# Second products by token tile at the end of the MLP, a new order in the first projections, and four steps to placing, in an attention and MLP kernel

## The chip, the cores and the metric

The kernel runs on one core of a Trainium2 chip. The metric is the device time of one execution in microseconds (us), taken as the median of the runs.

## The reference

A pre-norm attention layer with residual is followed by a pre-norm MLP with residual, for 2048 tokens of 512 features, 32 heads of 16 features, and 1792 hidden features.

```python
def _A_ref(x, wqkv, wo):
    qkv = (x @ wqkv).reshape(B, S, 3, H, Dh).transpose(2, 0, 3, 1, 4)
    q, k, v = qkv[0], qkv[1], qkv[2]
    scores = einsum("bhqd,bhkd->bhqk", q, k) * Dh ** -0.5
    p = softmax(scores, axis=-1)
    o = einsum("bhqk,bhkd->bhqd", p, v)
    return o.transpose(0, 2, 1, 3).reshape(B, S, D) @ wo

def _B_ref(x, w1, w2):
    h = silu(einsum("bsd,df->bsf", x, w1))
    return einsum("bsf,fd->bsd", h, w2)

h = x + _A_ref(layernorm(x), wqkv, wo)
h2 = h + _B_ref(layernorm(h), w1, w2)
```

## The kernel before

**Numbers.** Large products are made of fp16 halves: an operand is split in a high and a low part, and high by high, high by low and low by high are added in PSUM. So each product of 128 rows has three matmuls. The helpers are `mm` (L98, a matmul), `tr` (L101, a transpose on TensorE), `pool`, `act`, `dve` and `dma` (L105, L112, L115, L118: an operation on GpSimd, ScalarE, VectorE, and a DMA issued by SyncE); nearly every row of the profile has one of these lines, and the names of its tiles tell what it is. All of them keep the order of the program on their engine.

**Stages.** The first projections (0 to about 181 us) normalize the tokens in four blocks b of 512, project q and k (`project_qk`, L581) and v (`project_v`, L610, token tile by token tile of 128) and store q and k split, 48 rows for each head: `qs` for queries, `ks` for keys. Units of a block are n = 0 and 1 (k, then q, of two groups of heads) and n = 2 to 5 (token tiles of v). The weights' low parts (`wqk_l`, `wv_l`) are made by `split_qk` and `split_scaled` (L538) in between, the statistics and the norm of the next block by `statistics` and `normalize`.

Attention follows in 512 steps g. A step belongs to an item i = g // 16 (four heads and 512 queries), c = g % 16. It has four score matmuls (`scores`, L453: keys by queries, `ps<-qs,ks`), four exps on ScalarE (`pt<-ps`, 128 x 512), and the PV matmuls of the step two before (`values`, `ps<-pt,va`). The maximum of each query's scores is found ahead of the item: the scores of a later item are made the other way round (`ps<-ks,qs`) and reduced by VectorE (`mx`, L293 for one, L291 for a pair of banks), up to three maxima in a step, 64 for each item. `maxima(g)` (L1223) says how many a step gets, from the maxima still missing until each item begins; `BESIDE` (L72) says how many are made inside each of the three MLP blocks.

**Placing.** When the last maximum of a piece is found (`found_maxima`, L384), GpSimd splits the negative maxima in fp16 (`finish_max`, L300), and they are placed as two rows for each head into `qs`, which makes the score matmul subtract them. A piece is an item, or half of the last one: (31, 0) and (31, 1). If it is early enough, `place_far` (L330) does so `CALM` steps later: a DVE transpose `mt<-ns`, four DMAs to DRAM, and two DMAs `qs<-md`. Otherwise `place_max` (L342) does so two steps after: a transpose on TensorE into a bank of the scores, a DVE copy `mn<-ps`, and two DMAs `qs<-mn` (L354), both issued by SyncE. 27 pieces go the first way; items 8, 16, 24, 30 and both halves of 31 go the second.

**MLP.** The 2048 tokens go in four blocks of 512. Three are done inside the attention, ahead of steps 144, 272 and 400 (about 475 to 577, 838 to 941, 1199 to 1297 us), by `mlp` (L1043); the last after it, by `finish_last` (L1123, from about 1504 us). `mlp` makes 14 first products and gates (`gh`, `gl`), then for f = 0 to 13 the second products (`second`, L1023), four token tiles by three matmuls for each f. Bursts of scores for maxima lie inside (`BURSTS_2`, L84). In the last two f, the scores of the next two steps and, at the end of blocks 0 and 1, two single maxima are put between the products: three scores after 8 of the 12 products of f = 12, three after 2 of f = 13, and `last_scores` (L1057) after 10. Each token tile's last product is followed by its residual add on VectorE (`ot<-ps,factors,ot`) and its store. The very last token tile is added and stored in two halves of 256 columns.

The weights w1 and w2 of the last MLP block are loaded at c = 4 of item 31 (three `w<-w1d` and one `w<-w2d`, 256 KB each, by SyncE).

## Time and profile before

| | |
|---|---|
| Median of 3 runs | 1608.36 us (1607.56 to 1608.73) |
| Profiled execution | 1611.74 us |
| its span in the trace | 1609.9 us |
| mean granted clock of TensorE | 0.998 |
| TensorE busy | 1588.4 us, 99% |
| VectorE busy | 1391.9 us, 86% |
| ScalarE busy | 1208.2 us, 75% |
| GpSimd busy | 470.0 us, 29% |
| HBM traffic over the span | 74 GB/s |

Times in the trace are microseconds from the start of the span. PE stands for TensorE's matmuls, PEld for its weight loads, DVE for VectorE, ACT for ScalarE, POOL for GpSimd, and SP for SyncE, whose work here is to issue DMAs (SPq in rows; ACTq for DMAs that ScalarE issues). A row of a group of instructions names their line, engine, operation, and the tiles written and read. In the list of waits a row tells who waited for whom, the sum, the number of waits and the longest one. Matmuls that follow one another overlap in the rows by their pipelining, so starts are what to compare.

### The profile page before, as it was taken

Reading aid. Unit: us, or ns where it says so; the run is one execution under the profiler, and the core shown is the slowest. Engines: PE = TensorE matmul, PEld = TensorE weight load, DVE = VectorE, ACT = ScalarE, POOL = GpSimd, SP = SyncE. Lnnn points to the kernel's source line nnn. Section 1 sums busy time; section 2 is a strip of 40 time slices with the busy share of each in tenths; the row PEclk is TensorE's granted clock in tenths of the full one; section 3 lists DMA queues with packets and bytes.
Section 4 is the critical chain, followed back from the end, with each engine's and each line's share of the span. In section 5 each row is a group of like instructions: output and inputs, shape, how many; then the busy total and the mean of one; then the engine's idle time right before and its main releaser. Section 6 shows DMA issues by size and latency. Waiting matters only on the chain.

```text
span 1609.9 us, 28386 instructions
## 1 busy us (share of the span) xinstructions
PE 1588.4 (99%) x10526; PEld 476.3 (30%) x10526; DVE 1391.9 (86%) x2058; ACT 1208.2 (75%) x2384; POOL 470.0 (29%) x756
## 2 busy tenths in 40 slices
PE   9999999999999999999999999999999999999998
PEld 7434222222234322222233322222234322222253
DVE  7899999999989889999989889999977889998421
ACT  6545799999963079999964179999964099999632
POOL 4743544545426101211226101211127002111100
PEclk9999999999999999999999999999999999999999
DMA  5667533343323111121223111121223111101222
GB/s 197 183 163 235 135 86 96 111 122 96 102 65 103 53 52 37 44 51 33 62 63 98 60 52 36 41 52 36 57 71 109 47 52 36 34 12 24 70 86 72
DMA packets 105378, 126.13 MB, mean 78 GB/s; under 512 B 28464, under 2 KB 65392, under 8 KB 105240
## 3 DMA queue, kind: packets, MB, share of 16 engines
q1 hardware_dynamic: 100632, 115.93, 26.2%
q10 hardware_dynamic: 4608, 8.39, 2.0%
q8 instruction: 82, 1.34, 0.4%
q14 instruction: 56, 0.46, 0.1%
HBM read 93.67 MB, written 24.85 MB: 74 GB/s over the span
## 4 chain that ended last, share of the span: by engine, by line
PE 71%; ACT 19%; DVE 6%; DMA 2%; issue 1%; POOL 1%; SPq 0%; ACTq 0%; DVEq 0%; POOLq 0%
PE ps L98 70%; ACT pt L112 18%; DVE mx L293 2%; DVE mx L291 1%; PE ps L101 1%; DMA qd<-sh 1%; DVE ot L115 1%; DMA qs<-mn 1%; DVE pvs L115 0%; DVE htl L115 0%; SPq L118 0%; DVE st L115 0%; POOL rs L105 0%; DVE hx L115 0%; POOL ri L105 0%
## 5 line engine op out<-in xcount | busy, mean ns | idle before, releaser
L112 ACT ACTIVATE pt<-ps 128x512 f32<-128x512 f32 x2048 | 1010.4, 608 | 156.3 <-PE ps L98 155.7
L293 DVE TENSOR_REDUCE mx<-ps 128x1 f32<-128x512 f32 x1482 | 932.5, 684 | 49.2 <-PE ps L98 21.3
L98 PE MATMUL ps<-qs,ks 64*128 64x512 f16 x2048 | 531.9, 380 | 8.7 <-DMA qs<-mn 2.7
L98 PE MATMUL ps<-pt,va 128*17 128x512 f32 x4096 | 538.7, 599 | 1.4
L98 PE MATMUL ps<-ks,qs 48*128 48x512 f16 x2048 | 493.8, 380 | 1.8 <-DVE mx L291 1.6
L291 DVE TENSOR_REDUCE mx<-ps 128x2 f32<-128x1024 f32 x283 | 329.9, 1219 | 53.3 <-PE ps L98 52.2
L98 PEld LDWEIGHTS <-ks 64*128 64x128 f16 x2048 | 150.3, 95 | 554.9 <-issue 427.2
L105 POOL TENSOR_TENSOR ri<-rc,minus 128x16 f32<-128x16 f32 x31 | 90.7, 2927 | 263.8 <-DMA rc<-dn 248.2
L98 PE MATMUL ps<-w,gh 128*128 128x512 f16 x672 | 157.5, 380 | 0.7 <-ACT g L112 0.6
L98 PEld LDWEIGHTS <-qs 48*128 48x128 f16 x2048 | 125.2, 94 | 77.2 <-issue 63.7
L98 PEld LDWEIGHTS ps<-pt,va 128*17 128x17 f32 x4096 | 68.9, 95 | 222.8 <-issue 203.6
L98 PE MATMUL ps<-hth,w 128*128 128x512 f16 (+1 forms) x472 | 132.9, 369 | 0.0
L112 ACT ACTIVATE g<-ps,factors 128x512 f32<-128x512 f32 x56 | 38.4, 687 | 123.8 <-PE ps L98 96.7
L105 POOL TENSOR_TENSOR mx<-mx 128x32 f32<-128x32 f32 x54 | 13.0, 240 | 402.3 <-DVE mx L293 395.8
L98 PEld LDWEIGHTS <-w 128*128 128x128 f16 x708 | 66.3, 98 | 80.0 <-issue 12.4
L98 PEld LDWEIGHTS <-gh 128*128 128x128 f16 x672 | 61.3, 98 | 86.5 <-issue 20.2
L98 PE MATMUL ps<-htl,w 128*128 128x512 f16 (+1 forms) x236 | 84.0, 368 | 0.0
L115 DVE SCALAR_TENSOR_TENSOR gh<-g,factors,gh 128x512 f16<-128x512 f32 x14 | 10.5, 751 | 52.1 <-ACT gh L112 52.1
L112 ACT ACTIVATE ks<-ps 128x512 f32<-128x512 f32 x30 | 17.9, 598 | 50.1 <-PE ps L98 33.5
L105 POOL TENSOR_TENSOR sl<-ks,sh 128x512 f16<-128x512 f32 x30 | 35.3, 1179 | 52.2 <-ACT sh L112 24.6
L105 POOL TENSOR_TENSOR gh<-g,gh 128x512 f16<-128x512 f32 x42 | 48.5, 1155 | 3.5
L98 PE MATMUL ps<-xth,wqk_l 128*128 128x512 f16 x120 | 45.5, 379 | 0.8 <-DVE wqk_l L115 0.7
(153 smaller groups left out, 950.7 us busy)
## 6 DMA issues: line engine op xcount, KB each, us to landing
ks<-kd SPq DMA_DIRECT2D x120, 192.0 KB
w<-w1d SPq DMA_DIRECT2D x56, 256.0 KB
w<-w2d SPq DMA_DIRECT2D x56, 256.0 KB
ks<-in_B_w_dram ACTq DMA_DIRECT2D x28, 256.0 KB
w<-in_B_w_dram SPq DMA_DIRECT2D x28, 256.0 KB
qs<-qd SPq DMA_DIRECT2D x128, 48.0 KB
kd<-sh SPq DMA_DIRECT2D x16, 256.0 KB
qd<-sh SPq DMA_DIRECT2D x16, 256.0 KB
```

What stands on the lines that cost most here:

```text
L98: tc.keep_in_program_order(nc.tensor.matmul(*a, **k))
L101: tc.keep_in_program_order(nc.tensor.transpose(*a))
L105: tc.keep_in_program_order(getattr(nc.gpsimd, op)(*a, **k))
L112: pin(getattr(nc.scalar, fn)(*a, **k))
L115: pin(getattr(nc.vector, fn)(*a, **k))
L291: pin(nc.vector.tensor_reduce(of, space[:, n:n + 2, :], axis=AX.X, op=ALU.max))
L293: pin(nc.vector.tensor_reduce(of[:, j:j + 1], space[:, n, :], axis=AX.X, op=ALU.max))
```

## The change

It has six parts:

1. `CALM` goes from 6 to 4: a piece placed by way of DRAM is placed four steps after it was found.
2. In `place_max`, the second of the two DMAs is issued by ScalarE (`dma_beside`) in place of SyncE.
3. The second products of the last two f are made token tile by token tile (`last_seconds`): six matmuls for a tile, then its add and store, and so for four tiles. Four scores stand after the 6th product and four after the 18th, in four banks instead of three; the two single maxima of blocks 0 and 1 are left out. `finish_last` uses it too.
4. For the last token tile of all, the sum up to f = 11 is added to the residual early, and the last two f are made in two halves of 256 columns in banks of their own; the second half is stored by ScalarE's queue.
5. In the first projections of block 1, `wv`'s halves are split ahead of `project_qk`, after the norm's operations; `split_qk` there comes right behind `project_qk`, and elsewhere on GpSimd; in block 2 the statistics and the norm of tokens are spread differently over units 0 and 1. The bursts of maxima inside stand at other places, with one more pair, two maxima, in the projections (`BESIDE_V`, `BESIDE_V1`).
6. `BESIDE` goes from (138, 134, 110) to (136, 136, 110), and `BURSTS_2` from 16, 15, 14 to 16, 16, 14.

```diff
--- before.py
+++ after.py
@@ -66,22 +66,22 @@
 JOINT = 2
 AHEAD = 4
 FAR = 8
-CALM = 6
-
-
-BESIDE = (138, 134, 110)
+CALM = 4
+
+
+BESIDE = (136, 136, 110)
 OUTPUT = 9
 
-BESIDE_V = [(0, 0), (0, 4, 4, 4)], [(2, 2), (4, 4, 4, 4)], [(6, 6), (6, 6, 6, 6)]
-
-BESIDE_V1 = {4: 4}
+BESIDE_V = [(0, 0), (0, 0, 4, 4)], [(2, 4), (4, 4, 4, 4)], [(6, 6), (6, 6, 6, 6)]
+
+BESIDE_V1 = {(1, 1): {4: 4}, (1, 2): {4: 4}}
 
 BESIDE_A = {6: 6}
 
 BESIDE_A1 = 10, 9, 8, 7
 
 BURSTS_1 = ({f: 6 for f in range(FC) if f not in (6, 13)},) * 2 + ({f: 6 for f in range(FC) if f % 3},)
-BURSTS_2 = 16, 15, 14
+BURSTS_2 = 16, 16, 14
 SPAN_2 = 12 * (FC - 2)
 
 MORE = 2, 2, 0
@@ -113,6 +113,9 @@
 
     def dve(fn, *a, **k):
         pin(getattr(nc.vector, fn)(*a, **k))
+
+    def dma_beside(*a):
+        pin(nc.scalar.dma_start(*a))
 
     def dma(*a):
         pin(nc.sync.dma_start(*a))
@@ -351,7 +354,7 @@
         for j in range(2):
             dst = qs[i % RING][64 * j + 48:64 * j + 50, slice(None) if a is None else slice(a, a + 1)]
             dst = dst.rearrange("r a n -> r (a n)").rearrange("r (a b) -> r a b", b=P)
-            pin(nc.sync.dma_start(dst, mt[n // 2 * j:n // 2 * (j + 1), :]))
+            (dma_beside if j else dma)(dst, mt[n // 2 * j:n // 2 * (j + 1), :])
         placed.add(piece)
 
 
@@ -509,7 +512,7 @@
                 square_into(staged[n % 2], staged[n % 2], n)
             n = u - 5
             if 0 <= n < len(pieces):
-                act("dma_start", staged[n % 2], pieces[n])
+                dma_beside(staged[n % 2], pieces[n])
 
         def measure_rest():
             n = sum(PIECES)
@@ -611,7 +614,7 @@
             ps = bank()
             weave(product(ps, lambda c: xth[b][:, c, t * P:(t + 1) * P], lambda c: xtl[b][:, c, t * P:(t + 1) * P],
                           lambda c: wv_h[:, c, :], lambda c: wv_l[:, c, :], DC),
-                  {k: (lambda n=n: burst(n)) for k, n in BESIDE_V1.items()} if (b, t) == (1, 1) else {})
+                  {k: (lambda n=n: burst(n)) for k, n in BESIDE_V1.get((b, t), {}).items()})
             act("mul", va[:, 4 * b + t, :, 0:DH], ps.rearrange("p (h d) -> p h d", d=DH), v_f)
 
         def turn_x(b, t):
@@ -723,6 +726,8 @@
                 if b + 1 < NB:
                     rows = xts[b + 1]
                     stats, norm, turns = (other_ln if b else first_ln)[n]
+                    if b == 2 and n < 2:
+                        stats, norm = ((), (1,)) if n else ((0, 1), ())
 
                 def layer_norm():
                     for t in stats:
@@ -735,10 +740,12 @@
                 else:
 
                     layer_norm()
+                    if b == 1:
+                        half = slice(2 * n, 2 * n + 2)
+                        split_scaled(wv_h[:, half], wv_l[:, half], raw_v[:, half], v_w)
                     project_qk(b, k, scale=b > 0)
-                    if (b, n) in ((0, 1), (1, 0)):
-                        half = slice(2 * b, 2 * b + 2)
-                        split_scaled(wv_h[:, half], wv_l[:, half], raw_v[:, half], v_w)
+                    if (b, n) in splits:
+                        split_qk(splits.pop((b, n)))
                     if k == 0:
                         for i in range(2):
                             for h in range(4):
@@ -748,14 +755,16 @@
                 if b:
 
                     burst(BESIDE_V[b - 1][kind == "v"][n - 2 if kind == "v" else n])
-                if kind == "v":
+                if (b, n) == (2, 0):
+                    stats, norm = (2, 3), (0,)
+                if kind == "v" or (b, n) == (2, 0):
                     layer_norm()
                 for t in turns:
                     turn_x(b + 1, t)
                 if b == NB - 1 and n < DC:
                     split_x0(n)
                 if (b, n) in splits:
-                    split_qk(splits.pop((b, n)), "pool" if kind == "v" else "dve")
+                    split_qk(splits.pop((b, n)), "pool")
                 if b == 1 and n == 0:
                     load_x(3)
                 if b == 2 and n in (3, 5):
@@ -802,7 +811,8 @@
 
 
     idle_bank, last_bank = banks["st"]
-    lay_out(st=range(4), sm=(4, 5, last_bank))
+    attention_banks = 4, 5, last_bank, idle_bank
+    lay_out(st=range(4), sm=attention_banks[:3])
     pv = space[:, idle_bank, :]
     cpool = ctx.enter_context(tc.tile_pool(name="cpool", bufs=1, side="right"))
     bp = ctx.enter_context(tc.tile_pool(name="bp", bufs=PTS - EARLY))
@@ -1025,20 +1035,33 @@
         while f == 0 and len(acc) < 4:
             acc.append(bank())
         steps = (product(acc[t], lambda c: gh[:, t * P:(t + 1) * P], lambda c: gl[:, t * P:(t + 1) * P],
-                         lambda c: w2h, lambda c: w2l, 1, start=f == 0, stop=f == FC - 1) for t in range(4))
-        if f < FC - 1:
-            weave(chain.from_iterable(steps), inserts)
-            return
-        for t, step in enumerate(steps):
-            weave(step, {k - 3 * t: fn for k, fn in inserts.items()})
+                         lambda c: w2h, lambda c: w2l, 1, start=f == 0,
+                         stop=f == FC - 3 and 4 * b + t == KC - 1) for t in range(4))
+        weave(chain.from_iterable(steps), inserts)
+
+    def last_seconds(b, acc, gates, inserts={}):
+
+        w2 = [ws.pop(("w2", f)) for f in (FC - 2, FC - 1)]
+        k = 0
+        for t in range(4):
             n = 4 * b + t
-            h = rows_of(b, t)
-
+            h, rows = rows_of(b, t), slice(t * P, (t + 1) * P)
             parts = 1 + (n == KC - 1)
+            if parts == 2:
+                dve("scalar_tensor_tensor", h, acc[t], out_f, h, op0=ALU.mult, op1=ALU.add)
             for m in range(parts):
                 cols = slice(m * D // parts, (m + 1) * D // parts)
-                dve("scalar_tensor_tensor", h[:, cols], acc[t][:, cols], out_f, h[:, cols], op0=ALU.mult, op1=ALU.add)
-                dma(out[n * P:(n + 1) * P, cols], h[:, cols])
+                ps = acc[t] if parts == 1 else bank("sm")[:, cols]
+                first = True
+                for (gh, gl), (w2h, w2l) in zip(gates, w2):
+                    for x, w in ((gh, w2h), (gl, w2h), (gh, w2l)):
+                        mm(ps, x[:, rows], w[:, cols], start=first and parts == 2, stop=w is w2[1][1])
+                        first = False
+                        k += 1
+                        if k in inserts:
+                            inserts[k]()
+                dve("scalar_tensor_tensor", h[:, cols], ps, out_f, h[:, cols], op0=ALU.mult, op1=ALU.add)
+                (dma_beside if m else dma)(out[n * P:(n + 1) * P, cols], h[:, cols])
 
     def mlp(b):
 
@@ -1054,15 +1077,8 @@
             for _ in range(n):
                 scores(*ahead.pop(0), "sm")
 
-        def last_scores():
-
-            scores(*ahead.pop(0))
-            scores(*ahead.pop(0), "sm")
-            if b < 2:
-                singles(2)
-
         gates = []
-        lay_out(st=range(4))
+        lay_out(st=range(4), sm=attention_banks)
         for f in range(FC):
             tick()
             next_weights()
@@ -1077,12 +1093,15 @@
         act("activation", small.tile([P, 1], F32, name="sw"), ident[:, :1], AF.Exp)
         acc = []
         inserts = {SPAN_2 * (n + 1) // BURSTS_2[b]: lambda: burst(4, 4, 6) for n in range(BURSTS_2[b])}
-        inserts[12 * (FC - 2) + 8] = inserts[12 * (FC - 1) + 2] = lambda: some_scores(3)
-        inserts[12 * (FC - 1) + 10] = last_scores
-        for f in range(FC):
+        for f in range(FC - 2):
             tick()
             next_weights()
             second(b, acc, f, *gates[f], {k: inserts[12 * f + k] for k in range(1, 13) if 12 * f + k in inserts})
+        for _ in range(2):
+            tick()
+            next_weights()
+        last_seconds(b, acc, gates[-2:], {6: lambda: some_scores(4), 18: lambda: some_scores(4)})
+        lay_out(sm=attention_banks[:3])
 
     found = {}
 
@@ -1215,8 +1234,7 @@
             waiting.append((f, *gate(ps)))
             if f > 1:
                 second(b, acc, *waiting.pop(0))
-        while waiting:
-            second(b, acc, *waiting.pop(0))
+        last_seconds(b, acc, [gate for _, *gate in waiting])
 
     marks = [KC * (8 * b + 1) for b in range(1, NB)]
 
```

By these numbers the order of the work changes too, which the following rows show (a row has the line, the operation, the tile written, the tiles read, the shape, and a count where it repeats).

At the start of attention 216 maxima are done where it was 214, so some pieces are found a step earlier, the second half of item 31 at step 497 instead of 498, and placed at 499 instead of 500. SyncE's queue around that placing was, before:

```order
L118 DMA hx<-in_A_x_dram 128x512
L118 DMA rc<-dn 128x16
L118 DMA hx<-in_A_x_dram 128x512
L118 DMA w<-w1d 128x1024 x3
L118 DMA w<-w2d 128x1024
L354 DMA qs_102<-mn 2x4x128 x2
L118 DMA dr<-ri 128x16
```

and after, on SyncE:

```order
L121 DMA hx<-in_A_x_dram 128x512
L121 DMA rc<-dn 128x16
L121 DMA hx<-in_A_x_dram 128x512
L121 DMA qs_102<-mn 2x4x128
L121 DMA w<-w1d 128x1024 x3
L121 DMA w<-w2d 128x1024
L121 DMA dr<-ri 128x16
```

and the second of the pair, after, on ScalarE among the exps:

```order
L112 ACTIVATE pt<-ps 128x512 x44
L118 DMA qs_102<-mn 2x4x128
L112 ACTIVATE pt<-ps 128x512 x48
```

The pair moved ahead of the four weight loads, and its second part off that queue. The placing of item 7 moves from step 108 to 105, and that of item 15 from 235 to 233.

At the end of the first MLP block VectorE had three token tiles' adds (`ot`), two single reductions and the fourth tile's add, before:

```order
L291 TENSOR_REDUCE mx<-ps 128x2 x2
L115 SCALAR_TENSOR_TENSOR ot_1866<-ps,factors,ot_1866 128x512 x3
L293 TENSOR_REDUCE mx<-ps 128x1 x2
L115 SCALAR_TENSOR_TENSOR ot_1866<-ps,factors,ot_1866 128x512
L115 STREAM_TRANSPOSE mt<-ns 128x32
```

and after:

```order
L294 TENSOR_REDUCE mx<-ps 128x2 x3
L115 SCALAR_TENSOR_TENSOR ot_1869<-ps,factors,ot_1869 128x512 x4
L115 STREAM_TRANSPOSE mt<-ns 128x32
```

The single reductions are gone from between the adds. In the first projections, VectorE's row of work from the last low part of block 0 on (`sl`) was, before:

```order
L115 SCALAR_TENSOR_TENSOR sl<-ps,qk_82,sh 128x512
L115 SCALAR_TENSOR_TENSOR wv_l<-va,powers,wv_h 128x1024
L115 SCALAR_TENSOR_TENSOR wqk_l<-va,powers,wqk_h 128x4x128
L115 BN_STATS st<-ks_103 128x6
L115 BN_AGGR mv<-st 128x2
L115 BN_STATS st<-ks_103 128x6
L115 BN_AGGR mv<-st 128x2
L115 TENSOR_SCALAR ks_103<-ks_103,mv,rs 128x512
L115 SCALAR_TENSOR_TENSOR wv_l<-va,powers,wv_h 128x1024
```

and after:

```order
L115 SCALAR_TENSOR_TENSOR sl<-ps,qk_82,sh 128x512
L115 SCALAR_TENSOR_TENSOR wqk_l<-va,powers,wqk_h 128x4x128
...
L115 TENSOR_SCALAR ks_103<-ks_103,mv,rs 128x512
L115 SCALAR_TENSOR_TENSOR wv_l<-va,powers,wv_h 128x1024
...
L115 TENSOR_SCALAR ks_103<-ks_103,mv,rs 128x512
L115 SCALAR_TENSOR_TENSOR wv_l<-va,powers,wv_h 128x1024
L115 TENSOR_TENSOR xtl_129<-ps,xth_125 128x4x128 x2
```

What is left out there are two pairs of statistics (`BN_STATS`, `BN_AGGR`) each. Both halves of `wv_l` moved behind the statistics and the norm, and `wqk_l` ahead.

## Prediction

> **What bounds the kernel now.** I read in this order: the page's busy shares, the stretches of 20 us by engine, the waits, and then the timeline of TensorE around every stretch in which a step was long. The kernel loses little to see:
>
> ```profile
> PE 1588.4 (99%) x10526; PEld 476.3 (30%) x10526; DVE 1391.9 (86%) x2058; ACT 1208.2 (75%) x2384; POOL 470.0 (29%) x756
> ...
> 640.00:660.00 20.00, 20.00 (x158) 4.39 (x150) 19.04 (x32) 20.00 (x42) 5.85 (x13) 1.00 0.28 64
> ```
>
> The second row is a stretch in attention: its length and TensorE's busy time, then weight loads, VectorE, ScalarE and GpSimd, the granted clock, the DMA share and GB/s. (A row of a timeline has start, duration, engine, line, operation, count, and in brackets the idle time before it and its releaser; PEld is TensorE's weight load, SPq and ACTq are DMA issues.) TensorE and ScalarE are both full and VectorE nearly. No edit can shorten such a step; only places where a step is longer than this can give time. The usual step is 1.96 us (1305.31 − 1303.35, the first scores of two steps):
>
> ```profile
> 1303.35 0.39 PE L98 MATMUL ps<-qs,ks 64*128 64x512 f16 x1
> ...
> 1305.31 0.39 PE L98 MATMUL ps<-qs,ks 64*128 64x512 f16 x1
> ```
>
> So I went through the change by where steps exceed 1.96 us. The profiled execution took 1611.74 us, span 1609.9, hence 1.84 outside it; it stands 3.4 above the median of the runs, 1608.36. I work out a difference and subtract it from both.
>
> **Placing by PE transpose (items 8, 16, 24, 30).** Here the two qs<-mn transfers leave one after the other from SyncE, and a step is late:
>
> ```profile
> 426.95 0.39 PE L98 MATMUL ps<-qs,ks 64*128 64x512 f16 x1
> ...
> 429.43 0.39 PE L98 MATMUL ps<-qs,ks 64*128 64x512 f16 x1 [0.45 <-ACT pt L112]
> ```
> ```profile
> 426.95 0.09 PEld L98 LDWEIGHTS <-ks 64*128 64x128 f16 x1 [0.85 <-issue]
> ...
> 429.43 0.09 PEld L98 LDWEIGHTS <-ks 64*128 64x128 f16 x1 [1.37 <-DMA qs<-mn]
> ```
> ```profile
> PEld L98 <- DMA qs<-mn: 8.2, 5, 2.7
> ```
> ```profile
> 426.85 1.39 SPq L354 DMA_DIRECT2D qs<-mn  x2
> ```
>
> The step is 2.48, over by .52; the weight load says the same, 1.37 instead of .85. The last row of waits has five cases, the longest 2.7, so the others are (8.2 − 2.7)/4 = 1.37 each: four times .52 = **−2.08**. With the second transfer on ScalarE's queue, its issue starts with the first's and ends about .69 (1.39/2) sooner than SyncE's pair; that is more than .52, and the first transfer, unmoved, then ends in time. What ScalarE pays:
>
> ```profile
> 426.83 2.61 ACT L112 ACTIVATE pt<-ps 128x512 f32<-128x512 f32 x5
> ...
> 429.85 0.60 ACT L112 ACTIVATE pt<-ps 128x512 f32<-128x512 f32 x1 [0.41 <-PE ps L98]
> ```
> ```profile
> 43.60 0.59 ACT L112 CAST xth<-ps 128x512 f16<-128x512 f32 x1 [1.19 <-PE ps L101]
> 43.61 0.33 ACTq L112 DMA_DIRECT2D ks<-in_B_w_dram  x1
> 44.09 0.72 ACT L112 ACTIVATE wqk_h<-va,powers 128x512 f16<-128x512 f32 x1
> ```
>
> Behind the issue are queued the exps, and TensorE's fourth score of a step waits for them. The price lies between 0 (at 43.61 an issue on ScalarE lies beside a cast, and the next operation starts .49 after the cast, as exps do: 2.61/5 = .52) and .69 for each of six placings. I take .05 for five and .2 for the second half of item 31, near the row at 43.61: **+.45**. Ends for the four waits together: −2.08 and +2.1.
>
> A sentence of the Trainium skill speaks against this edit: "DMA: Bandwidth & Descriptors", Issuing engines are not separate DMA queues, has issuing on several engines save only the time to initiate, and its table calls two transfers to disjoint partition halves not worth it, since they serialize. By the first half the .69 of initiation is what is saved, as above; by the second, nothing. That second is a rival below, in this kernel's own terms.
>
> **Four steps to placing (CALM).** Two of the 27 pieces placed by DVE transpose are waited for:
>
> ```profile
> 397.46 0.09 PEld L98 LDWEIGHTS <-ks 64*128 64x128 f16 x1 [1.37 <-DMA qs<-md]
> ...
> 761.15 0.09 PEld L98 LDWEIGHTS <-ks 64*128 64x128 f16 x1 [1.69 <-DMA qs<-md]
> ```
>
> Over .85 these are .52 and .84: items 7 and 15, placed three and two steps sooner after the change (5.9 and 3.9 us). **−1.36.** The other end: placed sooner, the DVE transpose could now wait for GpSimd, with TensorE's score banks behind it:
>
> ```profile
> 384.63 0.22 POOL L105 TENSOR_TENSOR ns<-nm,ns 128x16 f16<-128x16 f32 x1
> ```
> ```profile
> 391.37 0.20 DVE L115 STREAM_TRANSPOSE mt<-ns 128x32 f16<-128x32 f16 x1
> ```
>
> GpSimd ends 6.5 us before; two steps (3.92) leave 2.6. So no stall; bounds −1.36 and −.5.
>
> **Item 31's second half.**
>
> ```profile
> 1489.70 0.21 DVE L115 COPY mn<-ps 16x128 f16<-16x128 f16 x1 [2.73 <-PE ps L101]
> ```
> ```profile
> 1491.11 1.38 SPq L118 DMA_DIRECT2D w<-w1d  x3
> 1492.53 0.43 SPq L118 DMA_DIRECT2D w<-w2d  x1
> 1493.06 1.39 SPq L354 DMA_DIRECT2D qs<-mn  x2
> ```
> ```profile
> 1498.17 0.78 PE L98 MATMUL ps<-qs,ks 64*128 64x512 f16 x4 [1.80 <-DMA qs<-mn]
> ...
> 1500.59 1.03 PE L98 MATMUL ps<-qs,ks 64*128 64x512 f16 x4
> ...
> 1502.97 0.39 PE L98 MATMUL ps<-qs,ks 64*128 64x512 f16 x2
> ```
> ```profile
> 1499.00:1502.50 3.50, 3.50 (x20) 0.30 (x14) 0.00 (x0) 2.93 (x7) 0.40 (x1) 0.51 0.41 116
> ```
>
> The rows are ready at 1489.91, yet their transfers are issued at 1493.06, behind four weight loads of 256 KB, and TensorE gets them at 1498.17; its weight load waited 2.71 instead of .85, so 1.86. Then the clock is at half (.51), and two steps take 2.42 and 2.38: .88 more. Found a step earlier, the piece is placed at step 499, ahead of the loads: issued by 1491.1 at the latest, it has over 5 us to the 1496.31 where TensorE wants it, and nothing 256 KB long before it. **−2.74**; ends: −2.74, as no more is lost there, and −.9, if half the wait stays and the half clock with it.
>
> Here too the Trainium skill has another rule: "TensorE: Matmul & The Clock Gate", Part 1, lets the clock fall to half only after an idle window of about 3.4 us. The trace doesn't agree, since .51 follows an idle of 1.80; by the rule the .88 would have another cause and stay, and the sum would be .88 less.
>
> **Ends of the three MLP blocks.** Block 0, from the first product behind the last burst to the next step's PV:
>
> ```profile
> 567.06 2.36 DVE L291 TENSOR_REDUCE mx<-ps 128x2 f32<-128x1024 f32 x2 [0.17 <-PE ps L98]
> ```
> ```profile
> 567.25 1.90 PE L98 MATMUL ps<-w,gh 128*128 128x512 f16 x8
> ...
> 576.75 1.05 PE L98 MATMUL ps<-pt,va 128*17 128x512 f32 x8
> ```
> ```profile
> 575.41 0.74 DVE L115 SCALAR_TENSOR_TENSOR ot<-ps,factors,ot 128x512 f32<-128x512 f32 x1
> ```
>
> That is 9.50 us now. Products stand (1.90 − .38)/7 = .217 apart. Afterwards: six products end the first tile at 568.33 + .22, two scores at 568.65; the second pair's bank waits for VectorE's two reductions, 567.06 + 2.36 = 569.42; products 7 to 18 run 569.78 to 572.4, four scores to 573.0, products 19 to 24 to 574.3. The fourth score of the next step waits for the last tile's add, 574.46 + .74 = 575.20, and PV follows at 575.60: −1.15. Block 1 the same, less one more burst of two pairs of slots (.63, by the same product pitch): −.52. Block 2:
>
> ```profile
> 1289.89 0.59 PE L98 MATMUL ps<-qs,ks 64*128 64x512 f16 x3 [0.41 <-DVE mx L291]
> ...
> 1296.49 1.05 PE L98 MATMUL ps<-pt,va 128*17 128x512 f32 x8
> ```
>
> The same way, with the seventh product at 1290.20, PV comes at 1295.99 instead of 1296.49: −.5. Together **−2.17**; ends −1.0 (the wait for the reductions twice in each block) and −2.8.
>
> **First projections.**
>
> ```profile
> 30.23 1.28 DVE L115 SCALAR_TENSOR_TENSOR wv_l<-va,powers,wv_h 128x1024 f16<-128x1024 f32 x1 [0.28 <-ACT wv_h L112]
> ...
> 34.42 1.28 DVE L115 SCALAR_TENSOR_TENSOR wv_l<-va,powers,wv_h 128x1024 f16<-128x1024 f32 x1
> ```
> ```profile
> 32.24 0.39 PE L98 MATMUL ps<-xth,wqk_l 128*128 128x512 f16 x1 [0.73 <-DVE wqk_l L115]
> ...
> 42.59 0.39 PE L98 MATMUL ps<-ks,qs 48*128 48x512 f16 x2 [0.57 <-DVE mx L291]
> ...
> 60.95 0.39 PE L98 MATMUL ps<-ks,qs 48*128 48x512 f16 x2 [0.74 <-DVE mx L291]
> ```
>
> VectorE did wv_l (1.28) ahead of wqk_l; without it the wait at 32.24 goes (.73, and the step to it). The two waits for mx go (.57 + .74), as the bursts stand further apart, over one more token tile of v. Against that, wv_l's second half now stands behind all four statistics and is ready about 37.5 instead of 35.7, while TensorE, earlier by 1.0, wants it about 35.8: a stall of 1.7. Pieces of −2.04, +1.7, and .22 for one more pair: I take **0**, since behind it VectorE is the bound up to the start of attention and takes up the difference. Ends −1.5 and +2.
>
> **The end.**
>
> ```profile
> 1603.24 2.85 DVE L115 SCALAR_TENSOR_TENSOR ot<-ps,factors,ot 128x512 f32<-128x512 f32 x5 [3.60 <-PE ps L98]
> ```
> ```profile
> 1605.88 0.90 SPq L118 DMA_DIRECT2D out_dram<-ot  x2
> ```
>
> The last add ends at 1606.09; SyncE's last two issues take .45 each, so the last starts at 1606.33, .25 behind the add. On ScalarE's queue it starts at once: **−.25** (ends −.5, and +.5 if halves cost TensorE more).
>
> **The sum**: −2.08 + .45 − 1.36 − 2.74 − 2.17 + 0 − .25 = −8.15; the profiled execution would take 1603.6, the median **1600.2**.
>
> **Rivals.**
> *The near waits stay* (the second transfer isn't what is late): the −2.08 goes and .45 with it: +1.6, 1601.8. For it: both halves share the DMA engines; against: issue alone takes .69 of a lateness of .52. .12.
> *The stall in the first projections halves the clock*, as 1.80 us of idle did at 1498.17: 1.75 us of waiting and then 3.4 us at half cost 1.7 beyond what VectorE's queue takes up: 1602.0. .11.
> *The second half of item 31 still comes late*, since its maxima aren't ready a step sooner, and the 2.74 stays: 1602.9. Against: with the added pair, 216 maxima instead of 214 are behind at the start of attention. .07.
> *The half clock has another cause*: 1601.1. .03.
> *ScalarE gives it back*: it is full (20.00 of 20), so waits removed from attention return as waits for exps; only the MLP ends and the last add are left, −2.4: 1605.9. Against: at 429.85 ScalarE itself idles .41 for this very wait. .08.
> *Slower: a DMA issue holds ScalarE until its transfer has landed.* From SyncE's issue at 426.85 to the end of TensorE's wait at 429.43 that is 2.58 us. The four near placings would then cost 2.58 − .52 each and the two of item 31 2.58 each, 13.4 in place of −1.63: 6.9 us slower than before, 1615.2. It loses from 1.4 us of holding on (6 × 1.4 against the 6.5 gained elsewhere and the 4 × .52 that goes). Against: at 43.61 an issue delayed nothing. .05.
> My forecast keeps .54.
>
> **How the numbers follow.** A run of this kernel can be told from no change at about .2%, 3.2 us. Faster by more (below 1605.1): .54 + .12 + .11 + .07 + .03 = .87; same .08; slower .05. The range takes in the forecast with its bounds and the first four rivals: 1598.0 (the first projections at their −1.5 and the MLP ends at −2.8) to 1605.0 (the near rival, the projections' +2 and the MLP ends at −1.0 together), and leaves out under .2.
>
> **What would show it.** Right: no waits of PEld for qs<-mn or qs<-md; the clock 1.00 through 1499 to 1503; the MLP ends at 8.4 us where 9.50 stood; steps of 1.96 where item 8's placing stood; attention starting within 1 us of before. Wrong: exps behind the ACTq transfer spaced by over .6; a wait for DVE wv_l near 36 followed by a clock below 1; a second wait for mx inside the last products; a DVE transpose waiting for GpSimd.

## The result and the profile after

The changed kernel takes **1605.75 us** in the median of 22 runs (1605.30 to 1606.21); the kernel before took 1608.32 in 22 runs beside it (1606.80 to 1609.80). The ratio is 0.9984 with a 95% interval of 0.9978 to 0.9991: 0.16% faster, 2.57 us, where 8.15 us were forecast and the range ended at 1605.0. The runs also became alike: their spread is 0.9 us where it was 3.0.

The profiled execution took 1605.79 us, beside the median. The first profile of before had taken 1611.74, so from profile to profile the gain is 5.95 us, more than twice that of the medians. This difference is the main question below.

The page of the changed kernel, its list of waits, and one stretch of 3.5 us (length and busy times by engine, then the granted clock):

```profile
span 1604.0 us, 28410 instructions
...
PE 1586.2 (99%) x10532; PEld 477.4 (30%) x10532; DVE 1392.9 (87%) x2056; ACT 1207.2 (75%) x2384; POOL 470.7 (29%) x756
```
```profile
PEld L98 <- DMA qs<-mn: 2.7, 3, 1.0
...
PEld L98 <- DMA qs<-md: 0.8, 1, 0.8
```
```profile
1499.00:1502.50 3.50, 3.27 (x24) 0.90 (x20) 2.30 (x7) 3.11 (x7) 1.26 (x1) 1.00 0.76 258
```

The waits for qs<-mn fell from 8.2 to 2.7 us: three are left, the longest 1.0, where a weight load waits .85 in any step. The clock in the stretch behind item 31's second half is 1.00 where it was 0.51. The placing there, on SyncE and TensorE:

```profile
1488.47 0.69 SPq L121 DMA_DIRECT2D qs<-mn  x1
1489.20 1.35 SPq L121 DMA_DIRECT2D w<-w1d  x3
```
```profile
1495.34 1.04 PE L98 MATMUL ps<-qs,ks 64*128 64x512 f16 x4
...
1497.31 1.04 PE L98 MATMUL ps<-qs,ks 64*128 64x512 f16 x4
```

The transfer goes ahead of the weights, and the steps are 1.97 apart. The end of the first MLP block:

```profile
567.72 1.47 PE L98 MATMUL ps<-w,gh 128*128 128x512 f16 x6
569.12 0.39 PE L98 MATMUL ps<-qs,ks 64*128 64x512 f16 x2
569.95 0.39 PE L98 MATMUL ps<-qs,ks 64*128 64x512 f16 x2 [0.44 <-DVE mx L294]
570.28 2.76 PE L98 MATMUL ps<-w,gh 128*128 128x512 f16 x12
...
576.13 1.05 PE L98 MATMUL ps<-pt,va 128*17 128x512 f32 x8
```

From the first product to PV it is 8.41 us where it was 9.50, with the wait for VectorE's two reductions where the forecast put it. Two rows of the first projections and of item 8's placing speak against the change:

```profile
37.79 0.38 PE L98 MATMUL ps<-wv_l,xth 128*128 128x512 f16 x1 [1.54 <-DVE wv_l L115]
```
```profile
426.80 1.52 ACTq L118 DMA_DIRECT2D qs<-mn  x1
428.38 1.08 ACT L112 ACTIVATE pt<-ps 128x512 f32<-128x512 f32 x2 [0.99 <-DVE mx L296]
```

The wait for wv_l's low part is there as worked out (1.54, forecast 1.7). At item 8 ScalarE's issue takes 1.52 us, and the next exp starts .99 late; the step from one PV to the next is 2.93 us instead of 2.48. At the five other placings the issue takes 0.62 to 0.65.

### The profile page after: what moved, and what is told of

Its sections match the earlier page's. It is cut to its first block, busy times and chain, and to the rows that moved or that the text cites. A ratio compares the mean times of both kernels' runs of the same rounds, so it can differ in the third digit from the quotient of the medians.

```text
span 1604.0 us, 28410 instructions
## 1 busy us (share of the span) xinstructions
PE 1586.2 (99%) x10532; PEld 477.4 (30%) x10532; DVE 1392.9 (87%) x2056; ACT 1207.2 (75%) x2384; POOL 470.7 (29%) x756
## 4 chain that ended last, share of the span: by engine, by line
PE 84%; ACT 8%; DVE 5%; issue 1%; DMA 1%; SPq 0%; POOL 0%; ACTq 0%; DVEq 0%
PE ps L98 83%; ACT pt L112 8%; DVE mx L294 2%; DVE mx L296 1%; PE ps L101 1%; DVE st L115 1%; DVE pvs L115 0%; DVE ot L115 0%; DVE htl L115 0%; DMA ks<-in_A_x_dram 0%; DMA w<-in_B_w_dram 0%; DVE hx L115 0%; SPq L121 0%; POOL rs L105 0%; DVE wv_l L115 0%
## 5 line engine op out<-in xcount | busy, mean ns | idle before, releaser
L98 PE MATMUL ps<-w,gh 128*128 128x512 f16 (+1 forms) x678 | 157.2, 378 | 0.7 <-ACT g L112 0.6
L98 PE MATMUL ps<-xth,wqk_h 128*128 128x512 f16 x120 | 45.8, 381 | 0.0
```

Source lines behind the costliest of these rows:

```text
L98: tc.keep_in_program_order(nc.tensor.matmul(*a, **k))
```

## The experiments

All are made of the kernel before or of the changed one by the edit shown. Each ran beside the kernel before, whose medians went from 1607.98 to 1608.86 us; so a difference of less than about half a us between two kernels that didn't run side by side isn't told from nothing. The steps of attention in the profiles, from one PV to the next, say more: between two profiles of the changed kernel (the second is in the last table) no step differs by more than .02 us, and only the start of attention moved, by .22.

Two theories stood against each other first. **A**: the first profile of before held waits that the usual execution doesn't have, so its terms can't be taken from the median. **B**: the waits are in every execution, and the changed kernel loses elsewhere what it gains.

**The kernel before again, two more profiles.** No edit.

> The kernel before, unchanged, profiled a second time. The first profiled execution took 1611.74 us, 3.4 above the median of 1608.32. Theory A: what was special in it is the wait for item 31's second half and the half clock behind it (1.86 + 0.88 us); then this profile takes about 1608.4, shows the step at item 31 without the 2.71 us weight-load wait, the clock at 1.00 through 1499 to 1503, and all other waits as before. Theory B: that wait is in every execution, and what was special is spread (a slower pace by some ns in every step); then the 2.71 us wait is here again and the other steps are shorter.

> The kernel before, unchanged, profiled a third time. In the second profile the step of item 31's second half was late by 0.46 where the first had 1.86 and 0.88 us behind it, and item 7's wait of 0.52 was not there. If such waits are a matter of the execution (theory A), the third profile again differs from both in one or more of them (items 7, 15 and 31), by a total that accounts for its distance in span from 1606.8; if the first profile was a single outlier (rival), this one repeats the second within 0.3 us.

The executions took 1608.61 and 1608.49 us. Item 31's second half in the second and then in the third profile of before, and the second's list of waits:

```profile
1495.98 0.79 PE L98 MATMUL ps<-qs,ks 64*128 64x512 f16 x4 [0.40 <-DMA qs<-mn]
...
1497.68 1.21 PE L98 MATMUL ps<-qs,ks 64*128 64x512 f16 x4
```
```profile
1495.88 0.78 PE L98 MATMUL ps<-qs,ks 64*128 64x512 f16 x4 [0.51 <-DMA qs<-mn]
```
```profile
PEld L98 <- DMA qs<-mn: 6.8, 5, 1.4
```

The wait is .40 and .51 where it was 1.80, and the half clock is gone. Item 7's wait differs too (the weight load waited 1.37 for qs<-md in the first profile, .94 in the second, 1.61 in the third):

```profile
396.76 0.09 PEld L98 LDWEIGHTS <-ks 64*128 64x128 f16 x1 [0.94 <-DMA qs<-md]
```
```profile
396.36 0.09 PEld L98 LDWEIGHTS <-ks 64*128 64x128 f16 x1 [1.61 <-DMA qs<-md]
```

The waits at items 8, 16, 24 and 30 were 2.47 to 2.48 steps in all three. Theory A, then: part of the waits are of the program, part of the execution. The third isn't just the second again, though their spans agree within 0.1: it starts the attention 1.1 us earlier and loses .67 of that at item 7.

**Only the weight loads moved.** The kernel before with

```diff
-            if c == 4:
+            if c == 5:
                 for f in range(3):
                     load_weights("w1", f)
```

> The kernel before, with the four weight loads of the last MLP block issued one step later (c = 5 in place of 4), so that they stand behind the placing of item 31's second half in SyncE's queue; nothing else moves. Theory A (the stall is rare or small in the usual execution): the median falls by 0 to 1.0 us, and the runs' spread, 3.0 us before, shrinks. Theory B (the stall is in every execution): the median falls by 2.7 us, to 1605.6.

Measured: 1607.63 us in 11 runs beside 1607.98, a ratio of 0.9998 (0.9989 to 1.0007). The steps at item 31's second half are all 1.96 in its profile:

```profile
1489.80 1.39 SPq L354 DMA_DIRECT2D qs<-mn  x2
1491.23 1.35 SPq L118 DMA_DIRECT2D w<-w1d  x3
```
```profile
1494.95 1.04 PE L98 MATMUL ps<-qs,ks 64*128 64x512 f16 x4
...
1496.91 1.04 PE L98 MATMUL ps<-qs,ks 64*128 64x512 f16 x4
```

Taking the whole wait away brings the median no more than the .35 by which the two differ, and that isn't told from nothing. The forecast's largest term, 2.74, was of one execution.

Item 15's wait is missing too in this profile. It was in all three of before (steps of 2.80, 2.79 and 2.91), but up to item 31 this is the same program, and it ran on the chip of the second profile. So such a wait comes and goes with the execution, on one chip. The weight load in the second profile of before, and here:

```profile
760.40 0.09 PEld L98 LDWEIGHTS <-ks 64*128 64x128 f16 x1 [1.69 <-DMA qs<-md]
```
```profile
759.83 0.09 PEld L98 LDWEIGHTS <-ks 64*128 64x128 f16 x1 [0.85 <-DMA qs<-md]
```

**Both transfers on SyncE again.** The changed kernel with

```diff
-            (dma_beside if j else dma)(dst, mt[n // 2 * j:n // 2 * (j + 1), :])
+            dma(dst, mt[n // 2 * j:n // 2 * (j + 1), :])
```

> The changed kernel with both of a near placing's transfers issued by SyncE again. If the second queue gains what was forecast, items 16, 24 and 30 are late by about 0.42 us each again and item 8, where ScalarE's issue took 1.52 us and cost 0.45 more than the old wait, gains 0.45: 1605.75 + 1.4 - 0.45 = 1606.7. If only the issue's hold of ScalarE matters (rival), no wait comes back and the time is 1605.2.

Measured: 1606.48 us (11 runs, 1606.02 to 1607.50), .73 above the changed kernel, nearer to the 1606.7 expected than to the rival. Items 16 and 24 are late again, by a step of 2.48 and 2.47 instead of 2.05 twice: the queue's gain is .43 each. At item 30 no step is longer than 1.99 here, where the changed kernel has one of 2.14: its rows are issued at 1442 in both where before had 1446.72, so it gains by being found sooner, and the second queue costs .18 there, behind ScalarE's issue. Item 8 did not gain .45:

```profile
429.47 0.39 PE L98 MATMUL ps<-qs,ks 64*128 64x512 f16 x1 [1.03 <-DMA qs<-mn]
```

Its step is 3.06, longer than with ScalarE's slow issue (2.93) and than before (2.48).

**The first of its form on ScalarE.** Item 8's second transfer back to SyncE, the later ones left:

```diff
-            (dma_beside if j else dma)(dst, mt[n // 2 * j:n // 2 * (j + 1), :])
+            (dma_beside if j and i > FIRSTS[0] else dma)(dst, mt[n // 2 * j:n // 2 * (j + 1), :])
```

> The changed kernel with item 8's second transfer issued by SyncE and all later ones by ScalarE. ScalarE's issue took 1.52 us at item 8 and 0.62 to 0.65 at the others. If the first such issue on ScalarE's queue is the slow one (theory A), item 16's now takes 1.5 us and that step is late instead of item 8's: 1606.2 to 1606.7. If the place is slow (rival), item 16 stays at 0.65 and item 8 waits for its second transfer as with one queue (about 1.1 us): within 0.3 us of 1605.75.

And one such transfer added ahead of the attention, whose data nothing uses:

```diff
         pool("memset", va[:, :, :, DH:DH + 1], 1.0)
+        mt = small.tile([32, P], F16, name="mn", bufs=1)
+        pool("memset", mt, 0.0)
+        to = small.tile([2, 16 * P], F16, name="to", bufs=1)
+        dma_beside(to.rearrange("r (a b) -> r a b", b=P)[:, :8], mt[16:32, :])
```

> The changed kernel with one more transfer of the near placings' form (16 rows of 128, from one tile to another) issued by ScalarE once before the attention, where ScalarE has time; its data are used by nothing. If the first issue of that form on ScalarE's queue is the slow one (theory A), the added issue takes 1.5 us, item 8's falls to 0.65 and its step loses its 0.9 us: 1604.85. If the slow one is the first after the attention's start, whatever came earlier (rival), item 8's stays at 1.52: 1605.75.

Measured: 1606.57 us (1606.29 to 1607.56), and 1605.42 (1604.78 to 1606.44). ScalarE's issues in the first, at item 16, and in the second, the added one and item 8's:

```profile
790.04 1.52 ACTq L118 DMA_DIRECT2D qs<-mn  x1
```
```profile
92.54 1.26 ACTq L118 DMA_DIRECT2D to<-mn  x1
```
```profile
426.29 0.65 ACTq L118 DMA_DIRECT2D qs<-mn  x1
...
427.00 2.56 ACT L112 ACTIVATE pt<-ps 128x512 f32<-128x512 f32 x5
```

The slow issue goes with being the first: it moves to item 16, whose step becomes 2.92, and with one sent ahead it is taken there, where ScalarE waits anyway; item 8's step falls from 2.93 to 2.05. The 32 transfers that ScalarE issued earlier in the changed kernel, of another form (a row of before shows one at 43.61, .33 us), did not do it. The median of the second kernel fell by .33, though, where .9 was expected; the two kernels didn't run side by side. What the added transfer is worth is measured once more below, under *Put together*.

**Six steps to placing again.** The changed kernel with `CALM = 6`.

> The changed kernel with six steps to placing again instead of four. By the first profile items 7 and 15 are late by 0.52 and 0.84 again: 1605.75 + 1.36 = 1607.1. By the later profiles of before such waits come in some executions and not in others (item 15's was missing in one, item 7's in two): 0 to 0.8 more, with a wider spread than the changed kernel's 0.9 us.

Measured: 1607.12 us (1606.62 to 1608.70), 1.37 above the changed kernel. In its profile item 7 alone accounts for it:

```profile
398.61 0.09 PEld L98 LDWEIGHTS <-ks 64*128 64x128 f16 x1 [2.20 <-DMA qs<-md]
```

The weight load waits 2.20 instead of .85, 1.35 more; item 15 isn't late. That the forecast's 1.36 comes out is luck: it was .52 and .84 there, it is 1.35 and 0 here, and both waits change with the execution. The spread is 2.1 us where the changed kernel's is 0.9.

**The MLP ends of before**, in the changed kernel: `second` and `mlp` as before with `last_scores` and `singles(2)`, `finish_last` without `last_seconds`, and

```diff
-BESIDE = (136, 136, 110)
+BESIDE = (138, 134, 110)
...
-BURSTS_2 = 16, 16, 14
+BURSTS_2 = 16, 15, 14
```

> The changed kernel with the ends of the MLP blocks of before: second products by f, scores in threes and twos, single maxima, one bank fewer, the whole last tile added in two halves from one bank, and the numbers of bursts and maxima of before. By the traces' terms (1.02 + 0.36 + 0.39 at the blocks and 0.3 at the end) the time rises by 2.1 us, to 1607.8; by the forecast's own terms by 2.4; if the gain at the blocks is given back by ScalarE within the next steps (rival), by under 0.8.

Measured: 1607.24 us (1606.80 to 1608.14): 1.49 more, between the 2.1 expected and the rival's .8. In the trace the blocks' ends take 1.11, .28 and .43 longer, the steps behind them .14, .14 and .05 less, and the end behind the last PV .17 longer.

**The last token tile of before**, in the changed kernel:

```diff
             for m in range(parts):
                 cols = slice(m * D // parts, (m + 1) * D // parts)
-                ps = acc[t] if parts == 1 else bank("sm")[:, cols]
...
-                (dma_beside if m else dma)(out[n * P:(n + 1) * P, cols], h[:, cols])
+                dve("scalar_tensor_tensor", h[:, cols], acc[t][:, cols], out_f, h[:, cols], op0=ALU.mult, op1=ALU.add)
+                dma(out[n * P:(n + 1) * P, cols], h[:, cols])
```

> The changed kernel with the very last token tile as before: its products in one bank of 512 columns, added and stored in two halves behind the last product, both stores issued by SyncE. By the traces the end is 0.3 us longer: 1606.05. If the early base add and the halves gain nothing (rival): 1605.75.

Measured: 1605.42 us (1605.09 to 1605.97). The .3 more didn't come. That the median is .33 lower isn't told from nothing by itself, as the kernels didn't run side by side; in the traces the old tile takes .17 less behind the last PV. VectorE's first and last adds at the end, in the changed kernel and then with the old tile:

```profile
1595.70 0.75 DVE L115 SCALAR_TENSOR_TENSOR ot<-ps,factors,ot 128x512 f32<-128x512 f32 x1 [1.66 <-PE ps L98]
...
1598.29 2.39 DVE L115 SCALAR_TENSOR_TENSOR ot<-ps,factors,ot 128x512 f32<-128x512 f32 x4 [0.55 <-PE ps L98]
```
```profile
1595.28 0.75 DVE L115 SCALAR_TENSOR_TENSOR ot<-ps,factors,ot 128x512 f32<-128x512 f32 x1 [1.66 <-PE ps L98]
...
1599.16 0.88 DVE L115 SCALAR_TENSOR_TENSOR ot<-ps,factors,ot 128x256 f32<-128x256 f32 x2 [0.54 <-PE ps L98]
```

From the first add's start to the last one's end it is 4.98 us with four adds in a row at the end, the early one among them, and 4.76 with the old tile, where VectorE still waits .54 for TensorE: the added operation is later than the products that it was to hide behind.

**wv's second half ahead of the statistics.** The changed kernel with

```diff
-                    layer_norm()
-                    if b == 1:
-                        half = slice(2 * n, 2 * n + 2)
+                    half = slice(2 * n, 2 * n + 2)
+                    if (b, n) == (1, 1):
+                        split_scaled(wv_h[:, half], wv_l[:, half], raw_v[:, half], v_w)
+                    layer_norm()
+                    if (b, n) == (1, 0):
                         split_scaled(wv_h[:, half], wv_l[:, half], raw_v[:, half], v_w)
```

> The changed kernel with the second half of wv split ahead of the statistics of its unit and not behind them, so that its low part is ready about 35.7 us and not 37.7. The 1.54 us wait of TensorE there goes. If VectorE is the bound behind it, as the forecast had it (a difference in arrival is taken up), the time stays within 0.3 us of 1605.75. If the arrival counts (rival), it falls by 0.7 to 1.5 us, to 1604.3 to 1605.0.

Measured: 1605.66 us (1605.28 to 1606.20), as the forecast's side expected. TensorE there:

```profile
36.18 0.38 PE L98 MATMUL ps<-wv_l,xth 128*128 128x512 f16 x1 [0.38 <-DVE wv_l L115]
...
38.22 0.66 PE L101 MATMUL ps<-ident,ks 128*128 128x128 f32 x4 [1.02 <-DVE ks L115]
```

The wait of 1.54 became one of .38 and, for the norm that VectorE now makes later, one of 1.02: it moved and didn't go.

**The first projections of before**, in the changed kernel (`BESIDE_V`, `BESIDE_V1` and the loop as before):

> The changed kernel with the first projections of before (two maxima fewer in them). The start of attention's PV comes 0.5 us earlier; item 31's second half is found a step later again and its first transfer stands behind the weight loads, item 30 is found a step later and waits unless the second queue frees it. If the two maxima are worth what they move (theory A): 1605.75 - 0.5 + 0.5 to 1.4 = 1605.8 to 1606.7. If the first projections' own 0.6 us is all that counts (rival): 1605.2.

Measured: 1605.70 us, but from 1604.63 to 1608.11. With two maxima fewer, item 31's second half stands behind the weight loads again; in the profiled execution its two steps were 2.57 and 2.31, .95 more than in the changed kernel. Against that stands a start of PV .55 earlier, and steps ahead of items 8, 16 and 24 that are .11 shorter each. Theory A's range begins at 1605.8, and the two profiles' spans are equal; the rival's 1605.2 isn't reached.

**Put together.** The first of these has the projections of before, the added transfer and `c == 5`; then, beside a second run of the changed kernel, the added transfer with the old last tile, and both of all.

> The changed kernel with the first projections of before, the added early transfer on ScalarE's queue, and the four weight loads of the last MLP block a step later (c = 5), so that item 31's second half stands ahead of them. If the terms add as the traces have them (0.55 at the start, 0.9 at item 8, nothing lost at item 31): 1605.75 - 1.45 = 1604.3. If ScalarE's pace takes part of it back (rival): 1605.0.

> The changed kernel, unchanged, a second time, on the same chip as the two that follow. Its earlier median was 1605.75 with a spread of 0.9. If the gain of the early transfer and of the old last tile (1605.42 each, measured on another call's chip) is real, this stands again at 1605.7; if 1605.4 is what that chip gives any of them (rival), this is 1605.4 too.

> The changed kernel with the early transfer on ScalarE's queue and the last token tile as before. If the two terms of the traces add (0.88 at item 8, and 0.17 to 0.27 behind the last PV step): 1604.6 to 1604.7. If the medians' own differences are all (0.33 each): 1605.1. If ScalarE takes the first back: 1605.5.

> The same as the last, with the first projections of before and the last MLP block's weight loads a step later. If the two orders of the first projections are equal, as forecast, 0.1 above the last, since item 30 is placed by the second queue at 0.09 (2.05 for 1.96): 1604.8, with a wider spread. If the new order costs 0.4 (the mean of the traces' starts of PV): 1604.3.

Measured:

| Kernel | Median of the runs | Runs | Against before |
|---|---|---|---|
| projections of before, added transfer, c = 5 | 1604.83 us (1603.20 to 1605.45) | 7 | 0.9972 (0.9961 to 0.9983) |
| changed kernel, second time | 1605.48 us (1605.29 to 1606.16) | 11 | 0.9982 (0.9973 to 0.9991) |
| added transfer, old last tile | 1604.57 us (1604.30 to 1605.20) | 11 | 0.9975 (0.9966 to 0.9984) |
| the same, projections of before, c = 5 | **1603.84 us** (1603.05 to 1604.30) | 7 | 0.9969 (0.9957 to 0.9980) |

The last three were measured together. The first ran at another time; it came out near its rival's 1605.0, and in its profile PV started at 182.61 us, later than in any other. The two suspects removed bring .91 (1.05 by the trace terms, .88 and .17). The profiles of these two kernels differ by −.87 at item 8, −.15 behind the last PV and +.12 at the start of PV, and nowhere else by more than .02 us: so the first transfer on ScalarE's queue and the new last tile are what cost the changed kernel this time.

The old order of the first projections, with the weight loads a step later, brings .73 more, further than either expectation. In the profiles .40 of it is the start of PV, which doesn't tell much: with the old order it stands between 180.17 and 182.61 us in seven profiles (mean 181.38), with the new one between 181.38 and 182.46 in nine (mean 181.70). The rest is in attention: with the new order a step ahead of each of items 8, 16 and 24 takes 2.07 in place of 1.96, and the blocks' ends are .14 longer together; with the old one the steps at item 30 are .11 longer together. The last version beats both kernels.

## Why the prediction was wrong, point by point

The step that failed is the one that took the profiled execution for every execution: "I work out a difference and subtract it from both". Here are the terms, with what the starts of PV in the traces give for them: the difference of the changed kernel's trace from the first and from the second profile of before (each column adds up to the difference of the spans). Of the 5.35 us between the forecast's sum and the last column, item 31's second half and item 7 make 2.8, item 8 makes 1.0, the ends of the MLP blocks .8, and the start of PV, which changes from execution to execution, .6.

| Part | Forecast | From the first | From the second |
|---|---|---|---|
| up to the start of PV | 0 | +.36 | +.62 |
| item 7 | −.52 | −.52 | −.08 |
| item 8 | −.47 | +.56 | +.56 |
| end of block 0 | −1.15 | −.87 | −.85 |
| item 15 | −.84 | −.83 | −.82 |
| item 16 | −.47 | −.42 | −.43 |
| end of block 1 | −.52 | −.21 | −.19 |
| item 24 | −.47 | −.32 | −.30 |
| end of block 2 | −.50 | −.32 | −.31 |
| item 30 | −.47 | −.53 | −.52 |
| item 31, first half and second placing | +.25 | +.17 | +.18 |
| item 31, second half | −2.74 | −2.66 | −.38 |
| behind the last PV | −.25 | −.34 | −.29 |
| sum | −8.15 | −5.93 | −2.80 |

(The forecast's +.45 for ScalarE stands with .05 at each of the four near items and .25 at item 31.)

- **What bounds the kernel, and where steps exceed 1.96 us**: right. All the time that was gained came from there. That 1605.75 lies beside the 1605.9 of the rival by which ScalarE gives everything back is luck: at items 16 and 24 the steps went from 2.48 to 2.05, and none of the six steps behind each became longer for it.
- **Item 31's second half**: the mechanism was right, for that execution to .08. But it was a transfer of a few KB behind 1 MB of weights, and how late it lands differs from execution to execution: 1.80, .40 and .51 us of waiting in three. The same for item 7, and for item 15, whose .84 was in three profiles of this program and not in a fourth. Items 31 and 7 make 2.7 of the 3.1 us between the first profile's span and the second's. The sign was to be seen: the profiled execution stood 3.4 us above the median of runs, and nothing was said of what those 3.4 were.
- **Items 8, 16, 24, 30**: −.43 each at 16 and 24 by the second queue, as forecast with its price for ScalarE. Item 30 gained by being found sooner. Item 8 failed: .56 lost where .47 was to be gained, 1.0 us; .45 of the .56 is the step with the slow issue, .11 a step ahead of it. The price of an issue on ScalarE was given from 0 to .69 and taken near the row at 43.61, which was of another form; the first of the new form takes 1.52. The table of the page "DMA: Bandwidth & Descriptors" of the Trainium skill, Rules for kernel authors, has transfers to two partition halves serialize. Its section Issuing engines are not separate DMA queues has several engines save the time to initiate. The gain of .43 at items 16 and 24, where the second issue started .74 after the first and now starts with it, agrees with the second of these.
- **CALM**: the mechanism was right, as the one weight load that still waits for qs<-md in the changed kernel does so for 0.8 us, as in any step. The size, −1.36 forecast and 1.37 measured by undoing it, is luck: the two waits together were 1.36, .9 and 1.7 us in the three profiles of before, .2 in that with the later loads, and 1.35 in the changed kernel with `CALM = 6`.
- **MLP ends**: the order of events was right to .1 us in block 0 (8.41 us, forecast 8.35). The rest of the shortfall, −1.35 for −2.17, comes in the step behind each block, where .05 to .15 is given back, and in the blocks themselves, which end 1.02, .36 and .39 earlier at PV than in the second profile, where 1.15, .52 and .50 were worked out.
- **First projections**: the stall of 1.5 at wv_l is there, the clock beside it stays at 1.00 (the rival falls), and moving wv_l brings nothing, as the forecast's zero had it. The order as a whole costs about .7, inside its bounds, but half of that lies in attention, of which the forecast had nothing.
- **The last tile**: the forecast's gap was there. The last store's issue starts .08 behind the last add, where it was .29 (the forecast read .25). What it left out is that the early add makes the adds end .18 later: counted from the last PV, the last issue ends at 90.32 us where it was 90.40, and with the old tile it would at 90.12. The rest of the .34 is the last store's landing, 2.90 where it was 3.15; in the profile with one queue, whose end is the same, that took 3.19, and nothing here tells why.
- **The half clock**: in the Trainium skill ("TensorE: Matmul & The Clock Gate", Part 1) it takes an idle window of about 3.4 us, free-running. These traces don't agree: one idle time of 1.80 was followed by .51, for 3.4 us. Idle times of 1.54 to 1.59 in front of wv_l, in nine profiles, were followed by none, as the one at 37.79; no run here tells what decides between.

Left open: why item 8's second transfer, issued by SyncE, is .58 later in the changed kernel than in before (steps of 3.06 in two kernels, 2.48 in before); whether the .40 at the start of PV is of the new order at all; and why the steps ahead of items 8, 16 and 24 are longer with it.

## What to carry to other kernels

Before terms are summed from one profile, ask how far that execution stands from the median of the runs: what is above it is made of waits that others don't have, and a wait for a small transfer behind large ones is the first suspect. A second profile of the same kernel costs one run and shows most of them; item 15's wait here was missing only in the fourth. A wait that varies also shows in the spread of the runs, which here went from 3.0 to 0.9 us while the median moved by 2.6; with `CALM = 6` alone it was 2.1 again.

## What the runs showed of the hardware

The first DMA of a form that ScalarE issues held it for 1.52 us at a busy place, 1.26 at an idle one, and the next ones .62 to .65; it was the same at item 8 and at item 16. At item 8 the next exp started .99 late. One such transfer sent ahead moves the .87 to where the engine waits anyway. Whether it is the form, or any transfer between tiles, wasn't tried.

Executions of one program repeat closely: in the profiles of before, the only steps of attention that differ by more than .03 us are those that wait for a small transfer at items 7, 15 and 31 and, in one, those at the half clock behind such a wait. Beside them the start of attention differs, by up to 1.35 us.
